# A clustered attention and MLP kernel: single entries for small instructions, constant products at the start, q's scale on VectorE, and another order

## The chip, the cores and the metric

The kernel runs on one core of a Trainium2 chip. The metric is the device time of one execution in microseconds (us), lower is better. The engines are TensorE (PE, products into PSUM), VectorE (DVE), ScalarE (ACT), GpSimd (POOL) and SyncE (SP, which here issues all DMAs). Each takes its instructions in the order in which the program issued them.

## The reference

```python
q_n, k_n, c_n = each row / (norm + 1e-6)
q_assign = argmax(q_n @ c_n.T); k_assign = argmax(k_n @ c_n.T)     # 16 centroids per head
scores = q @ k.T / sqrt(64), -1e9 where q_assign != k_assign
attn = softmax(scores); out = attn @ v                             # 4 batches, 8 heads, 768 rows, 64 columns
x = out as 3072 x 512
h = x @ w_in                                                       # 512 x 2048
g = (a0 + a1 h + a2 h^2 + a3 h^3) / (1 + |b0||h| + |b1| h^2 + 1e-6)
return g @ w_out                                                   # 2048 x 512
```

The MLP weights arrive as 64-bit floats, which the kernel unpacks itself (lines 517 to 562).

## The kernel before

Work is in *pairs* of heads, four pairs in each of four batches, 16 pairs in all. Each number is split into a high and a low float16 part, so that products keep their precision. A Python class `Plan` collects every step as a closure with its engine (`op(...)`), and a list `ORDER` of 4218 indices says in which order the closures are called. As each engine works in order, that list fixes every queue, and with it which buffer of a ring is given to whom. One closure may issue several instructions; between these nothing else can stand.

The steps that matter here:

- `prep` (line 885 on), for each pair: load q and k (`rq`, `rk`), sum of squares on ACT (`tk`, `tq`, with an accumulator), a transpose on PE (`kt`, `qt`, L949), a maximum over the partitions on DVE (`km`, `qm`, L951), a product with ones that spreads it (`kb`, `qb`, L953), then scales that are powers of two: `k_scale` (three DVE instructions, L963 to L971), `q_scale` (L963), `q_scale2` (three one-column instructions L979, L980, L982; on DVE for the first pair, on POOL for the 15 others), and a reciprocal (L993). With them ACT makes the high part and DVE the low part (L1012) of k and q. A transposing DMA (L1028) brings `tk` and `tq` to `sk` and `sq`. Then the logits against the centroids (`ptl`, L1060), the assignments (L1074 to L1084) and their marks (L1089, L1102), which are transposed too.
- Batch 0 goes key-major (`attend_keys`): 12 score blocks per pair (`s`, L1288), each followed by a maximum on DVE (`top`, L1297); when all are there, the row maxima are written in parts (`parts`, L1307 to L1314), `q2` is transposed again, second products `z` (L1332) follow, exponentials on ACT (`at`), products with v (`px`, L1351, which read `rv`), sums (L1357), a newton step (`newton`, two DVE instructions), a spread (L1385).
- Batches 1 to 3 (`attend`): scores (`s`, L1164), scale and maximum on DVE (L1193), exponential on ACT, high part on ACT, low part on DVE (`ah`, L1224), a transposing DMA, products with v (`px`, L1244).
- The MLP (`moe`): first product `ph` (L1453), the rational function on ACT, DVE and POOL, second product `po` (L1602). `g_scale` makes its column scales from 36 small instructions on DVE, POOL and ACT, bound into 10 entries.
- `v_scale` loads v (`rvm`, shared ring of two with the raw weights), squares it on ACT and makes one scale per batch (`vt`, `vb`). `rv` is v once more, in a ring of two buffers; in batch 0 a buffer is free when PE has read it for the last `px` of its pair.
- PSUM: the small products take their tiles from a ring of two (`misc`).

Of the kernel before, what the change touches and what calls it, by code (L numbers as in the profile page):

```python
# [18 lines left out]
P = 128  # L19
# [38 lines left out]
K = {'xn': 14, 'scp': 1, 'vsc': 0.75, 'sup0': 0, 'stk': 2, 'lop': 0, 'mgp': 0, 'rvn': 2, 'at': 3, 'vn': 3, 'ah': 5, 'sua': 1.0, 'T1': 1, 'quick': 1, 'sqd': 0.0, 'gld': 0.0, 'gp': 0.3, 'pp': 0.0, 'NR': 19, 'acb': 1.0}  # L58
# [3 lines left out]
3 4 5 6 7 8 9 377 376 379 381 382 383 40 41 42 43 388 44 28 32 29 30 31 33 391 392 45 374 375 380 384 385 386  # L62
10 387 389 390 34 35 36 37 38 394 395 46 47 11 393 489 490 398 492 50 48 49 51 494 495 496 501 70 71 72 74 396
73 399 400 401 402 403 397 39 52 404 405 407 406 488 487 493 497 498 88 92 89 53 54 90 504 505 76 77 78 79 499
500 502 91 93 80 55 56 57 503 507 508 64 67 68 81 58 408 506 509 409 414 415 82 83 12 13 61 62 69 63 59 430
431 84 418 419 510 86 85 87 60 75 410 411 424 425 432 433 412 413 428 429 420 421 511 512 513 514 14 0 601 378
16 600 15 17 18 19 422 423 416 417 515 516 426 427 434 603 602 605 607 608 609 65 517 518 520 614 94 95 606
118 122 119 120 519 96 97 98 99 20 21 22 112 116 610 23 611 121 113 114 612 613 615 616 617 618 115 117 123
103 104 435 436 437 440 441 453 454 438 439 455 456 442 443 521 619 522 535 536 620 621 622 623 109 130 131
132 715 124 125 126 127 128 129 106 134 133 527 528 529 530 110 111 444 445 446 447 135 107 24 25 26 541 542  # L70
470 471 100 624 625 626 713 716 718 448 449 27 627 628 629 105 450 457 458 533 534 537 538 136 137 630 525 526
1 714 172 173 176 719 160 164 108 631 632 635 66 633 161 162 459 723 724 138 139 140 141 460 174 472 473 539
540 145 142 151 152 101 102 531 532 175 177 720 721 725 726 523 524 163 545 546 543 544 722 727 547 146 147
# [12 lines left out]
301 303 295 674 675 676 271 296 297 277 268 269 270 582 1272 687 688 700 702 701 703 689 690 774 775 776 304
305 777 322 323 324 326 306 307 308 309 325 327 334 335 336 364 691 316 692 319 320 310 311 778 338 2 337 365
693 313 339 781 704 677 705 706 707 779 780 1274 1273 1275 1276 366 367 1277 1278 340 341 342 343 782 1398
1397 1403 1407 328 329 330 792 793 344 345 1279 1280 1281 331 794 1402 708 709 710 783 368 795 694 784 332 333
785 796 797 278 1229 1230 369 798 799 809 810 1404 1405 1406 811 786 787 1408 1409 370 371 321 228 346 347 788  # L90
789 813 1410 1411 1412 348 349 812 350 351 1413 1414 790 1401 1284 1282 361 358 1231 1232 362 363 312 565 317
318 791 372 373 678 800 801 814 802 803 815 816 355 1233 1234 1283 1285 1289 1290 1291 1539 1297 1298 1299 804
805 806 1292 1293 1300 1301 817 1235 1236 1237 1238 1239 1240 1294 1295 1302 1303 1313 1314 1241 818 1242 819
820 1416 1540 1541 1415 1417 1418 1419 1545 1542 1544 359 1315 1316 1317 1305 1306 1420 1421 1549 352 1318
1319 821 822 823 2228 1258 2229 279 275 276 314 315 1307 826 827 828 1308 829 832 833 1333 1334 1335 1309 1310
1422 830 831 1243 842 843 844 360 1311 1312 1423 1426 1320 1304 1296 1427 1424 1425 1546 1547 845 846 1336
1337 1325 1326 847 848 849 834 807 835 836 272 695 858 1548 1550 1551 273 356 357 837 838 839 1286 1327 1338
1339 1340 859 860 861 862 1552 863 850 864 1328 1329 865 808 851 852 874 875 1555 876 877 1341 1342 853 878
854 855 1330 1331 1343 880 879 1553 1554 1287 891 892 893 1344 894 1345 1346 840 1349 1350 1351 1352 1556 1347
1428 1353 1354 895 896 881 882 866 1684 1355 1356 2230 841 907 908 909 910 867 353 897 856 1361 1362 1363 1369  # L100
1370 1288 1321 1322 1323 1364 1371 868 911 912 857 1365 1366 1372 913 869 870 1373 1374 883 884 354 923 924
925 926 929 898 899 1367 1375 1324 1377 1378 1379 1385 1386 1387 1244 871 873 927 928 1380 1381 1388 1389 914
915 599 885 886 1348 1245 1246 933 1247 887 930 1382 1383 888 1390 1391 1332 1357 1358 1359 1360 900 916 940
941 942 943 946 2231 3222 3223 1431 1432 1439 1440 1441 944 917 945 1557 1558 1683 1682 1559 1560 1392 901 931
918 1561 1433 1434 1435 902 947 948 1442 1443 919 920 903 904 1436 1437 1444 1445 872 889 960 961 963 962 932
934 964 976 977 979 978 966 1562 967 1447 1448 1449 1450 982 983 965 980 1451 1455 1456 890 906 981 1368 1384
3224 1681 1376 1393 1394 1452 1453 935 936 937 1457 968 1458 1459 1563 1467 1468 1248 969 970 1686 1395 1396
1460 1461 1462 971 1564 1446 1454 1438 824 1469 993 994 996 1470 995 1471 949 972 973 997 1472 1473 998 1429
1565 1568 1569 2232 1430 3225 999 1000 905 1687 1009 1010 1011 1012 1483 1484 1485 1475 1476 1477 1013 1014
950 1486 1478 1479 1487 951 1691 952 953 1015 1016 1480 1481 922 921 1688 1689 1488 1489 1490 984 1001 938  # L110
1041 1042 1044 1043 1002 1491 1492 1493 1494 1045 986 985 987 1003 1495 1496 939 1503 1504 1505 1506 1249 1017
1046 1051 1497 1004 1047 1048 954 956 1463 1464 1465 1507 1508 1018 1690 1692 1693 1250 1511 1512 1513 1566
1567 1474 1482 2233 1509 1543 1514 1695 1005 988 989 990 1006 1466 1515 1516 1058 1059 1519 1520 1019 1517
1521 1522 1523 1696 955 958 1524 1525 1025 1026 1027 1060 1061 1028 1573 1574 1575 1576 1062 1251 1252 1064
1065 1694 1020 1031 1032 1577 1578 974 1527 1528 1063 825 1579 1029 1030 975 992 991 1007 1581 1582 1049 1697
1033 1034 1035 1529 1530 1531 1698 1036 1583 1584 1585 711 712 1685 957 1498 2253 1510 2254 1499 1500 1501
1502 1253 1021 1022 1532 1533 1586 1587 1074 1075 1076 1077 1078 1079 1080 1081 1050 1066 1094 1589 1095 1096
1097 1590 1591 1597 1598 1599 1600 1067 1699 1700 1701 1702 1592 1518 1526 1098 1703 1023 1008 1052 1053 1570
1571 1593 1037 1038 1068 1601 1054 1055 1704 1594 1595 1602 1603 1099 1534 2256 2252 1604 2251 1111 1112 1114
1113 1117 1118 1617 1618 1619 1620 1609 1610 1611 1024 1535 1536 1040 1057 1069 1621 1115 1070 1071 1100 1116  # L120
1612 1613 1705 1622 1623 1580 1596 1588 1624 1614 1615 1082 1083 1084 1712 1713 2257 1537 1633 1634 1635 1636
1119 2258 2259 1085 1706 1707 1708 1538 1572 1637 1638 1039 1625 1626 2260 2262 1710 959 1639 3226 1640 1627
1628 1629 1086 1087 1120 1121 1630 1631 2265 1073 1127 1128 1129 1133 1130 1645 2261 1646 1056 1647 1653 1654
# [1569 lines left out]
```

## Time and profile before

| | us |
|---|---|
| median of 3 runs | 914.93 (914.34 to 915.98) |
| the profiled execution | 914.8 |
| its span, first to last instruction | 913.0 |
| PE busy | 854.0 |
| DVE busy | 820.1 |
| ACT busy | 790.7 |
| POOL busy | 576.6 |

The span is the time from the first instruction to the last; the execution has 1.8 us around it. Busy times are sums over stages with different limits, so that the stages are read one by one.

### The profile page before, as it was taken

To read this page: it belongs to the slowest core of one execution; us is meant where nothing else is said; L and a number is where in the kernel's file an instruction comes from. 1 tells how busy PE (TensorE), PEld (TensorE's weight loads), DVE (VectorE), ACT (ScalarE), POOL (GpSimd) and SP (SyncE) were. 2 spreads that over 40 slices of the span, in tenths; PEclk is the share of its full clock that TensorE was granted. 3 is DMA by queue.
4 is the path that set the end of the run, shared out by engine and by line. 5 is a ranking of instruction groups with operands and counts; after the bars stand their busy time and mean duration, and the time that the engine had idled before them with its cause. 6 is when DMAs were issued, how large, how long until landed. Compare 5 with 4: busy or idle time off the path is not lost.

```text
span 913.0 us, 20529 instructions
## 1 busy us (share of the span) xinstructions
PE 854.0 (94%) x7705; PEld 584.9 (64%) x7705; DVE 820.1 (90%) x1538; ACT 790.7 (87%) x1486; POOL 576.6 (63%) x607
## 2 busy tenths in 40 slices
PE   1779998988999999999999999999999999999998
PEld 1456766765666766667666765776766566776663
DVE  6868888679999999999999999999999998887784
ACT  5576878999999999999999989999999798985662
POOL 3537767779675757458654765447756554668675
PEclk9979999999999999999999999999999999999999
DMA  8997784878959898997999779888987596320000
GB/s 229 237 204 175 174 197 142 191 184 148 184 122 196 142 202 180 195 172 131 215 160 203 156 126 187 162 163 149 189 179 136 96 199 105 70 47 1 36 24 23
DMA packets 360852, 137.70 MB, mean 151 GB/s; under 512 B 335664, under 2 KB 352048, under 8 KB 360752
## 3 DMA queue, kind: packets, MB, share of 16 engines
q1 hardware_dynamic: 360752, 136.39, 74.5%
q8 instruction: 60, 0.98, 0.4%
q14 instruction: 40, 0.33, 0.1%
HBM read 41.98 MB, written 6.29 MB: 53 GB/s over the span
## 4 chain that ended last, share of the span: by engine, by line
PE 53%; DVE 15%; ACT 15%; DMA 9%; issue 5%; SPq 1%; POOL 1%; ACTq 0%; DVEq 0%
PE po L1602 18%; PE ph L1453 17%; PE s L1164 6%; PE px L1244 5%; ACT s L397 4%; DMA sq<-tq 3%; DVE s L1193 3%; ACT ah L397 2%; ACT u L397 2%; DVE ah L1224 2%; DMA rvm<-in_v_dram 2%; PE z L1332 1%; ACT t L397 1%; DVE g L1553 1%; PE ptl L1060 1%
## 5 line engine op out<-in xcount | busy, mean ns | idle before, releaser
L1602 PE MATMUL po<-wout,g 128*128 128x512 f16 x1152 | 266.7, 379 | 0.5 <-POOL g L1591 0.3
L1453 PE MATMUL ph<-x,win 128*128 128x256 f16 x2304 | 266.3, 273 | 0.6 <-DVE df L1075 0.4
L1453 PEld LDWEIGHTS <-win 128*128 128x128 f16 x2304 | 223.6, 98 | 41.7 <-DVE t L1478 1.7
L1602 PEld LDWEIGHTS <-g 128*128 128x128 f16 x1152 | 111.2, 98 | 121.3 <-issue 2.2
L1591 POOL TENSOR_TENSOR g<-t,u 128x512 f16<-128x512 f32 x84 | 117.6, 1402 | 97.1 <-DVE t L1584 81.1
L1193 DVE TENSOR_SCALAR_CACHE_REDUCE s<-s,cc 128x768 f32<-128x768 f32 x144 | 144.7, 1018 | 4.2 <-PE s L1164 3.7
L1224 DVE SCALAR_TENSOR_TENSOR ah<-s,su,ah 128x768 f16<-128x768 f32 x144 | 143.4, 1009 | 3.9 <-ACT ah L397 3.4
L1518 POOL TENSOR_TENSOR s<-s,u 128x512 f32<-128x512 f32 x84 | 112.5, 1344 | 49.5 <-ACT s L397 38.8
L397 ACT ACTIVATE s<-s,nm 128x768 f32<-128x768 f32 x144 | 126.0, 876 | 12.3 <-DVE s L1193 10.4
L397 ACT ACTIVATE ah<-s,su 128x768 f16<-128x768 f32 x144 | 127.0, 898 | 10.3 <-DVE su L1212 9.4
L1164 PE MATMUL s<-sk,sq 128*128 128x384 f16 x576 | 114.2, 326 | 11.7 <-DVE ah L1224 9.2
L1164 PEld LDWEIGHTS <-sq 128*128 128x128 f16 x576 | 53.0, 97 | 52.6 <-DVE ah L1224 17.4
L1244 PE MATMUL px<-at,vhi 128*64 128x256 f16 x864 | 73.9, 275 | 1.0 <-DVE t L1478 0.6
L397 ACT ACTIVATE t<-ph,gk 128x512 f32<-128x512 f32 x84 | 65.2, 779 | 3.7 <-PE ph L1453 3.7
L1471 DVE SCALAR_TENSOR_TENSOR t<-ph,gk,t 128x512 f32<-128x512 f32 x84 | 62.3, 742 | 4.8 <-ACT t L397 3.3
L1572 DVE SCALAR_TENSOR_TENSOR s<-s,g 128x512 f32<-128x512 f32 x84 | 64.6, 769 | 0.7
L1478 DVE SCALAR_TENSOR_TENSOR t<-t,gk,ph 128x512 f32<-128x512 f32 x84 | 62.3, 742 | 1.3
L397 ACT ACTIVATE s<-u,g 128x512 f32<-128x512 f32 x84 | 60.6, 724 | 1.1 <-POOL t L1578 0.3
L397 ACT ACTIVATE u<-s,cq 128x512 f32<-128x512 f32 x84 | 59.7, 718 | 1.7 <-POOL s L1518 1.7
L1244 PE MATMUL px<-at,vlo 128*64 128x256 f16 x432 | 59.6, 273 | 0.0
L397 ACT ACTIVATE u<-ph,gk 128x512 f32<-128x512 f32 x84 | 57.4, 688 | 1.4 <-PE ph L1453 0.9
L1553 DVE SCALAR_TENSOR_TENSOR g<-t,gk,u 128x512 f16<-128x512 f32 x61 | 53.5, 878 | 4.1 <-ACT u L397 3.9
(227 smaller groups left out, 1543.2 us busy)
## 6 DMA issues: line engine op xcount, KB each, us to landing
rwi<-in_moe_w_in_dram SPq DMA_DIRECT2D x16, 512.0 KB, 3.7
rwo<-in_moe_w_out_dram SPq DMA_DIRECT2D x16, 512.0 KB, 4.8
rk<-in_k_dram SPq DMA_DIRECT2D x32, 192.0 KB, 3.6
rq<-in_q_dram SPq DMA_DIRECT2D x32, 192.0 KB, 3.7
rvm<-in_v_dram SPq DMA_DIRECT2D x16, 384.0 KB, 4.3
rv<-in_v_dram SPq DMA_DIRECT2D x16, 384.0 KB, 4.4
out_dram<-ob SPq DMA_DIRECT2D x24, 256.0 KB, 3.1
sk<-sk SPq DMA_DIRECT2D x12, 192.0 KB, 3.5
```

The source lines that it names most:

```text
L397: lambda: nc.scalar.activation(out=out(), in_=in_(), func=func, **{a: (x() if callable(x) else x) for a, x in kw.items()}),
L1164: nc.tensor.matmul(sc.ap[:, i, :SH], lhsT=st["q" + x].ap[:, j, t, :], rhs=st["k" + x].ap[:, j, ks, :].rearrange("p t c -> p (t c)"), start ...
L1193: lambda nm=nm, view=view: ts(out=view(), in0=view(), scalar1=cc.ap[:, 0:1], scalar2=None, op0=ALU.mult, op1=ALU.min, accum_out=nm.ap),
L1224: lambda part=part, view=view, su=su: stt(out=part(1), in0=view(), scalar=su.ap, in1=part(0), op0=ALU.mult, op1=ALU.subtract),
L1244: nc.tensor.matmul(px.ap[j * D : (j + 1) * D, :], lhsT=vv.ap[:, j, kt, :], rhs=at[j].ap[:, p_, kt].rearrange("p t c -> p (t c)"), start=(i ...
L1453: nc.tensor.matmul(ph.ap[:, fi * TW : (fi + 1) * TW], lhsT=win[:, wpart, c, f * P : (f + 1) * P], rhs=xs[c].ap[:, xpart], start=(i == 0), ...
L1471: lambda t=t, h=h, ph=ph, col=col: stt(out=t[h].ap, in0=ph.ap, scalar=col("rho")(), in1=t[h].ap, op0=ALU.mult, op1=ALU.mult),
L1518: lambda uv=uv, sv=sv: nc.gpsimd.tensor_tensor(out=sv(), in0=sv(), in1=uv(), op=ALU.mult),
L1553: lambda tv=tv, uv=uv, col=col, g16=g16: stt(out=g16(0), in0=tv(), scalar=col("a0")(), in1=uv(), op0=ALU.add, op1=ALU.mult),
L1572: lambda sv=sv, g16=g16: stt(out=sv(), in0=sv(), scalar=1.0 + 1e-6, in1=g16(0), op0=ALU.add, op1=ALU.mult),
L1591: lambda tv=tv, uv=uv, g16=g16, e=(nc.vector if kshare("gld", b, i_) else nc.gpsimd): e.tensor_tensor(out=g16(1), in0=tv(), in1=uv(), op=A ...
L1602: nc.tensor.matmul(po[ti].ap, lhsT=g16(gg)[:, c0 : c0 + P], rhs=wout[:, wpart, f, :], start=(i == 0 and f == 0), stop=(i == 2 and f == NF ...
```

## The change

`ORDER` has 4446 entries instead of 4218. 212 come from splitting: `scales`, `bound1`, `square_term`, `root`, `bound3`, `bound4`, `columns` (in `g_scale`), `k_scale`, `q_scale2`, `fixed_rows`, `mark`, `parts` and `newton` were closures with two to ten instructions and are now one entry for each instruction. 16 are new: `warm`, eight products of a constant 128 x 128 tile with itself into a tile of the `misc` ring, which nobody reads. `q_scale2` goes to DVE for all 16 pairs. The list is another one throughout.

```diff
-K = {..., 'acb': 1.0}
+K = {..., 'acb': 1.0, 'warm': 16, 'fast': 16}
...
+    w16w = cp.tile([P, P], BF16, name="w16w")
+    nc.vector.memset(w16w, 1.0)
...
+    def warm(vt):
+        wm = misc([P, 2 * TW], F32, f"warm{vt}")
+
+        def spin():
+            for _ in range(8):
+                nc.tensor.matmul(wm.ap[:, :P], lhsT=w16w, rhs=w16w, start=True, stop=True)
+
+        op("PE", 433, spin, [], [wm], vt)
...
-        def q_scale2():
-
-            pts = ts if quick else nc.gpsimd.tensor_scalar
-            pts(out=qs.ap[:, 1:2], in0=ks.ap[:, 1:2], scalar1=2.0 ** -21, scalar2=1.0, op0=ALU.mult, op1=ALU.mult)
-            pts(out=qs.ap[:, 0:1], in0=qs.ap[:, 0:1], scalar1=2.0 ** 61, scalar2=qs.ap[:, 1:2], op0=ALU.mult, op1=ALU.max)
...
-        if quick:
-            op("DVE", 480, q_scale2, [ks], [qs, cc], u, n=3)
-        else:
-            op("POOL", 1635, q_scale2, [ks], [qs, cc], u)
+        fast = b * NPAIR + hp < kn("fast", 1)
+        pts = ts if fast else nc.gpsimd.tensor_scalar
+        op(
+            *(("DVE", 481) if fast else ("POOL", 1631)),
+            lambda: pts(
+                out=qs.ap[:, 1:2], in0=ks.ap[:, 1:2], scalar1=2.0 ** -21, scalar2=1.0, op0=ALU.mult, op1=ALU.mult
+            ),
+            [ks], [qs], u,
+        )
...
-            dve(1200, newton, [px], [rw], ux, [rwc])
+            dve(
+                1201,
+                lambda px=px, rw=rw, rq=rq: stt(
+                    out=rw.ap[:, P:], in0=px.ap[:, 1, :P], scalar=eps, in1=rq(), op0=ALU.add, op1=ALU.mult
+                ),
+                [px], [rw], ux, [rwc],
+            )
...
+    for i in range(int(kn("warm", 0))):
+        warm(-40 + 0.01 * i)
```

How the first entries of some queues read in the two lists (pair numbers after the names; halves of q and k are loaded one by one):

```
SP before:   centroids, k0, k0, w_in, w_in, q0, q0, w_in, w_in, k1, k1, transpose k0, w_out, transpose q0
SP after:    q0, v (rvm0), q0, w_in, centroids, k0, k0, w_in, w_in, w_out, transpose k0, w_in, transpose q0, k1
rv before:   pair 0, 1, 2, 3 of batch 0       rv after: pair 0, 3, 1, 2
ACT before:  centroid norm, square k0, w_in, w_in, scale k0, square q0, ...
ACT after:   square v (rvm0), square q0, w_in, square k0, centroid norm, w_in, scale k0, ...
PE before:   kt0 kb0 qt0 qb0 centroids kt1 kb1 ptl0 w_in qt1 w_in qb1, scores of pair 0
PE after:    8 warm, qt0, 2 warm, kt0 kb0 qb0 centroids, 2 warm, ptl0, 2 warm, kt1 kb1 qt1 qb1 w_in w_in,
             7 scores of pair 0, 2 warm, 5 scores of pair 0
```

## Rows read from the trace of the kernel before

**Rows 1.** Stretch, length; busy PE, PEld, DVE, ACT, POOL (xcount); PE clock, DMA share, GB/s.

```profile
0.00:60.00 60.00, 29.76 (x225) 19.58 (x226) 44.33 (x118) 34.02 (x60) 26.93 (x45) 0.89 0.95 231
60.00:240.00 180.00, 164.25 (x1937) 119.34 (x1937) 151.96 (x298) 156.12 (x295) 134.83 (x155) 1.00 0.75 173
240.00:800.00 560.00, 551.32 (x4826) 376.97 (x4821) 541.28 (x1029) 532.61 (x1027) 337.33 (x351) 1.00 0.86 160
800.00:900.00 100.00, 100.00 (x688) 65.33 (x687) 78.17 (x90) 66.72 (x105) 74.70 (x56) 1.00 0.09 25
900.00:913.00 13.00, 8.68 (x41) 3.72 (x38) 4.38 (x6) 1.26 (x2) 2.77 (x3) 0.91 0.11 40
```

**Rows 2.** PE's waits, longest first, in 0-60, 60-240, 240-800: us, times, longest.

```profile
PE kt L949 <- ACT tk L397: 14.6, 3, 5.4
...
PE s L1164 <- DVE ah L1224: 3.3, 4, 1.5
...
PE s L1164 <- DVE ah L1224: 5.8, 7, 1.7
```

**Rows 3.** Chain of waits: start, us, what.

```profile
55.27 6.76 PE z L1332 x36
```

**Rows 4.** `kt` on PE: two instructions (start, us), then all 16 (ns min/median/max).

```profile
5.32 0.37 PE L949 MATMUL kt<-ident,sumk 128*1 128x128 f32 x1 [5.32 <-ACT tk L397]
...
48.29 0.37 PE L949 MATMUL kt<-ident,sumk 128*1 128x128 f32 x1 [3.85 <-ACT tk L397]
...
L949 PE MATMUL kt<-ident,sumk x16: 270/272/372, 5.3 to 663.8; 128*1 128x128 f32 x16
```

**Rows 5.** Stages as in rows 1: the start, and around 50 us.

```profile
4.00:8.00 4.00, 0.95 (x3) 0.57 (x3) 2.88 (x14) 2.16 (x4) 0.00 (x0) 1.00 0.92 325
48.00:56.00 8.00, 5.68 (x31) 4.29 (x32) 4.28 (x19) 5.50 (x12) 1.80 (x4) 0.50 1.10 211
```

**Rows 6.** DVE in order of time, around the first maximum of a score block.

```profile
32.83 0.34 DVE L1019 COPY tq<-tq 128x768 f16<-128x768 f16 x1
33.51 0.96 DVE L1297 TENSOR_REDUCE top<-s 128x1 f32<-128x768 f32 x1 [0.33 <-PE s L1288]
34.79 0.96 DVE L1297 TENSOR_REDUCE top<-s 128x1 f32<-128x768 f32 x1 [0.32 <-PE s L1288]
```

**Rows 7.** ACT in order of time: one exponential of `z`.

```profile
57.99 0.90 ACT L397 ACTIVATE at<-z,cc 128x768 f32<-128x768 f32 x1 [0.38 <-PE z L1332]
```

**Rows 8.** The three scale instructions by line: ns min/median/max, first and last start.

```profile
L979 POOL TENSOR_SCALAR qsc<-ksc x15: 190/192/515, 27.2 to 670.1; 128x1 f32<-128x1 f32 x15
L979 DVE TENSOR_SCALAR qsc<-ksc x1: 144/144/144, 12.8 to 12.8; 128x1 f32<-128x1 f32 x1
...
L980 POOL TENSOR_SCALAR qsc<-qsc x15: 291/295/904, 29.6 to 670.4; 128x1 f32<-128x1 f32 x15
...
L980 DVE TENSOR_SCALAR qsc<-qsc x1: 214/214/214, 13.0 to 13.0; 128x1 f32<-128x1 f32 x1
...
L982 POOL TENSOR_SCALAR cc<-qsc,ksc x15: 260/265/697, 30.3 to 670.8; 128x1 f32<-128x1 f32 x15
L982 DVE TENSOR_SCALAR cc<-qsc,ksc x1: 213/213/213, 13.3 to 13.3; 128x1 f32<-128x1 f32 x1
```

**Rows 9.** All waits, longest first: that of POOL before L980.

```profile
POOL qsc L980 <- DVE qsc L963: 14.5, 6, 4.0
```

**Rows 10.** PE in order of time: three reads of `rv`.

```profile
90.25 2.81 PE L1351 MATMUL px<-at,rv 128*64 128x256 f32 x24
...
125.58 2.81 PE L1351 MATMUL px<-at,rv 128*64 128x256 f32 x24
...
140.53 2.81 PE L1351 MATMUL px<-at,rv 128*64 128x256 f32 x24
```

**Rows 11.** DMA issues (the page): KB each, us to landing.

```profile
rv<-in_v_dram SPq DMA_DIRECT2D x16, 384.0 KB, 4.4
```

**Rows 12.** SP's queue in order of time.

```profile
95.00 3.93 SPq L411 DMA_DIRECT2D rwi<-in_moe_w_in_dram  x2
```

More of the change, by code (lines that the diff above doesn't have):

```diff
@@ L869, in g_scale, with pts1 @@
-        dve(590, scales, [wie, ev], [gk, g1], vt, n=2)
-        op("POOL", 1820, bound1, [aab], [g1], vt)
-        dve(160, bound2, [], [g1], vt)
-        op("POOL", 1300, square_term, [aab], [g1], vt)
+        def pts1(ns, out, in0, s1, s2, op0, op1, r=(), w=None):
+            op(
+                "POOL", ns,
+                lambda: pts(out=out(), in0=in0(), scalar1=s1() if callable(s1) else s1, scalar2=s2() if callable(s2) else s2, op0=op0, op1=op1),
+                list(r), w or [g1], vt,
+            )
@@ new lines, in G, with A @@
+        def G(i):
+            return lambda: g1c(i)
+        def A(i):
+            return lambda: ac(i)
+        MU, AD, MX = ALU.mult, ALU.add, ALU.max
+        dve(591, lambda: ts(out=kk["rho"](), in0=wi_e, scalar1=ev.ap[:, 0:1], scalar2=None, op0=MU), [wie, ev], [gk], vt)
+        dve(592, lambda: nc.vector.tensor_reduce(out=g1c(HB), in_=kk["rho"](), axis=AX.X, op=MX), [gk], [g1], vt)
+        pts1(1821, G(HB), G(HB), 4.0 * math.sqrt(H) * TOP * TOP, 1.0, MU, MU)
+        pts1(1822, G(D1), G(HB), A(5), A(4), MU, AD, [aab])
@@ L874, in g_scale @@
         act(250, lambda: g1c(R1), lambda: g1c(R1), AF.Exp, [], [g1], vt, scale=0.5)
-        dve(1700, root, [], [g1], vt, n=4)
-        op("POOL", 1460, bound3, [aab], [g1], vt)
-        dve(1330, bound4, [woe], [g1], vt, n=5)
-        op("POOL", 3400, columns, [ab, aab, woe], [gk, g1], vt)
+        dve(1701, lambda: nc.vector.reciprocal(out=g1c(BT), in_=g1c(R1)), [], [g1], vt)
+        dve(
+            1702, lambda: stt(out=g1c(R1), in0=g1c(BT), scalar=g1c(X1), in1=g1c(R1), op0=MU, op1=AD), [], [g1], vt,
+        )
@@ new lines, in g_scale @@
+        pts1(1822, kk["sg"], lambda: wo_e, G(HB), TOP, MU, MU, [woe, g1], [gk])
+        pts1(1821, G(OI), G(OI), 1.0 / TOP, 1.0, MU, MU)
+        pts1(1822, G(BT), G(BT), A(4), 1.0, MU, MU, [aab])
+        pts1(1822, kk["kap"], kk["rho"], G(R1), 1.0, MU, MU, [g1], [gk])
+        op("POOL", 1823, lambda: ptt(out=kk["sr"](), in0=kk["sg"](), in1=kk["rho"](), op=MU), [], [gk], vt)
+        for name, src, i in (("a2", "sr", 2), ("a1", "sr", 1), ("a0", "sg", 0), ("a3r", "sr", 3)):
+            pts1(1822, kk[name], kk[src], lambda i=i: ab.ap[:, i : i + 1], 1.0, MU, MU, [ab], [gk])
@@ L881, in clustered_attention_moe_kernel @@
+        op("POOL", 1823, lambda: ptt(out=kk["a3r"](), in0=kk["a3r"](), in1=kk["rho"](), op=MU), [], [gk], vt)
     xt = {}
@@ L987, in prep @@
[L987 to L992 removed]
+        dve(146, q_scale, [qsum], [qs], u)
+        dve(536, lambda: half_exponent(ks.ap[:, 0:1], pb.ap), [pb], [ks], u)
+        dve(
+            537,
+            lambda: ts(
+                out=ks.ap[:, 0:1], in0=ks.ap[:, 0:1], scalar1=2.0 ** 62, scalar2=2.0 ** -60, op0=ALU.mult, op1=ALU.max
+            ),
+            [], [ks], u,
+        )
@@ new lines, in prep @@
+        dve(538, lambda: nc.vector.reciprocal(out=ks.ap[:, 1:2], in_=ks.ap[:, 0:1]), [], [ks], u)
+        fast = b * NPAIR + hp < kn("fast", 1)
+        pts = ts if fast else nc.gpsimd.tensor_scalar
+        op(
+            *(("DVE", 481) if fast else ("POOL", 1631)),
+            lambda: pts(
+                out=qs.ap[:, 1:2], in0=ks.ap[:, 1:2], scalar1=2.0 ** -21, scalar2=1.0, op0=ALU.mult, op1=ALU.mult
+            ),
+            [ks], [qs], u,
+        )
+        op(
+            *(("DVE", 482) if fast else ("POOL", 1632)),
+            lambda: pts(
+                out=qs.ap[:, 0:1], in0=qs.ap[:, 0:1], scalar1=2.0 ** 61, scalar2=qs.ap[:, 1:2], op0=ALU.mult, op1=ALU.max
+            ),
+            [], [qs], u,
+        )
@@ L993, in prep @@
+        op(
+            *(("DVE", 483) if fast else ("POOL", 1633)),
+            lambda: pts(
+                out=cc.ap[:, 0:1], in0=qs.ap[:, 0:1], scalar1=ks.ap[:, 0:1], scalar2=QSC if keymajor else -QSC,
+                op0=ALU.mult, op1=ALU.mult,
+            ),
+            [qs, ks], [cc], u,
+        )
         dve(157, lambda: nc.vector.reciprocal(out=qs.ap[:, 1:2], in_=qs.ap[:, 0:1]), [], [qs], u)
@@ L1043, in rows @@
                 return tm[x].ap.rearrange("p h t d -> p (h t) d")[:, :, P - NCL :]
-            def fixed_rows():
-                nc.gpsimd.tensor_copy(out=rows("k2"), in_=mrow.unsqueeze(1).broadcast_to([P, 2 * NT, NCL]))
-                nc.gpsimd.memset(rows("q2"), 0.0)
-            op("POOL", 1100, fixed_rows, [], [tm["k2"], tm["q2"]], vt + kb("p2", b, 2))
+            op(
+                "POOL", 1101,
+                lambda: nc.gpsimd.tensor_copy(out=rows("k2"), in_=mrow.unsqueeze(1).broadcast_to([P, 2 * NT, NCL])),
+                [], [tm["k2"]], vt + kb("p2", b, 2),
+            )
+            op("POOL", 1102, lambda: nc.gpsimd.memset(rows("q2"), 0.0), [], [tm["q2"]], vt + kb("p2", b, 2))
         for x in ("k1", "q1"):
```

132 lines of the change are left out of this document (64 added, 68 removed), and 376 rows, old and new, of the table ORDER.

## The prediction

> **What bounds the kernel now.** I read the busy times by stage first, then what TensorE (PE) waits for in each stage, then single instructions where a wait has to be priced. By the stage table [rows 1] PE is busy 29.76 of the first 60 us, 164.25 of the next 180, 551.32 of the 560 after that, all of 800 to 900, and 8.68 of the last 13. So its idle time is 30.2 + 15.8 + 8.7 + 0 + 4.3 = 59 us of 913. From 240 us on PE is the bound; an order can only win what PE idles, or bring the dense part forward. The same rows show how little room the other engines have there: VectorE (DVE) is busy 541.28 and ScalarE (ACT) 532.61 of 560 us.
>
> What PE waits for differs by stage [rows 2]: in the first 60 us for the squares of q and k on ACT, whose input is a load; from 60 to 240 and from 240 to 800 most of all for DVE (row `ah`). The first dense PE work, the second products `z` of pair 0, starts at 55.27 us [rows 3]; everything before it is a chain of load, scales, transposing DMA, 12 scores with a maximum each, and one more transposing DMA.
>
> **The change part by part.**
>
> *Separate entries.* The same instructions are issued, so nothing is added; what is gained is that another instruction may stand between two of them. Alone: 0. It only matters through the order, below.
>
> *Constant products.* 16 entries of 8 products of 128 columns, 128 in all. In PE's new queue 8 groups stand ahead of the first real work, the rest at places 9, 10, 15, 16, 18, 19, 33 and 34, so the last two lie among the first scores. They take no engine but PE, which idles half of that stretch [rows 1], so their own time costs 0; two groups among scores that wait for a 0.95 us maximum each cost at most 1 us. Where a group takes a PSUM buffer of the ring of two, it waits for the reader of that buffer: the group at place 19 waits until DVE has read the logits of pair 0, and the transposes of pair 1 (`kt`) wait behind it. Pair 1 has the room, since its scores begin after pair 0's.
>
> What they can give is clock. The granted clock is recorded as 1.00 in the first 44 us, but `kt` took 0.37 us at 5.32, the same as at 48.29, where the recorded clock is 0.50 (1.2 GHz), against a median of 272 ns over all 16 [rows 4, 5]. By the durations PE ran at 1.2 GHz at the start, by the recorded clock at 2.4. On the path to the first scores the slow rate costs: DVE idles 0.33 + 0.32 us for PE before the first two maxima [rows 6], and the small products ahead of them about 0.1 us each, some five of them, so about 1.2 us in all. Bounds: 0, if the clock falls back in the long waits that stay between the groups and the scores, and 1.2, if it stays up. I take 0.6, because the last groups stand right at the scores but most run before 8 us. The second slow stretch, 0.50 from 48 to 56 us [rows 5], costs ACT 0.38 us before each of three exponentials (one of them in [rows 7]), 1.1 us; no group stands near it, so I take 0 and keep 1.1 for the range.
>
> The Trainium skill ("TensorE: Matmul & The Clock Gate", section "What's actually happening") says that the array's default state is the throttled clock and that activity releases it. By that page the 1.00 at the start is no granted level but a missing record, and the groups lift the clock. By the recorded 1.00 the whole term would be 0 and the sum 0.6 us higher; by the durations it is as taken.
>
> *q's scale.* For 15 of 16 pairs three one-column instructions leave POOL (192 + 295 + 265 ns) and go to DVE (144 + 214 + 213 = 571 ns) [rows 8]. DVE gets 15 x 0.571 = 8.6 us more. POOL loses 11.3 us and, more, the 14.5 us for which it stood before the second of the three until DVE had made its input [rows 9]. POOL is busy 337 of 560 us in the dense part [rows 1], so I book nothing for that. On DVE at most the 12 pairs of batches 1 to 3, 6.9 us, fall into 240 to 800, where it idles 18.7 us. Bounds: 0, if they all fall into holes, and +6.9, if DVE's queue is what PE waits for throughout. PE's waits for DVE there are 5.8 us of 8.7 [rows 2], but 5.8 us in 560 is rare; I take +0.5.
>
> *The new order, start.* In SP's queue the load of q and the first load of v for the scale of v come first, then w_in, centroids, and k; before, it was centroids, k, w_in, q. ACT's first entry becomes the square of v. So k's square, which sets off k's scale, comes later by the two loads that now precede it, q's earlier, and one 384 KB load is gone from the stretch after 30 us. DVE has 52 instructions ahead of its first maximum before (33.51 us) and 53 after: three scale instructions of pair 1 more (0.57 us), against a copy (0.34 us, as the one in [rows 6]) and the two short instructions of a weight block's scale (about 0.3 us) that move behind it. That is a draw, and DVE, busy 44 of these 60 us [rows 1], paces the stretch. The moved ones then lie between the first maximum and the last part of the row maxima, 0.65 us. I take 0, with 2.5 us either way: the 0.65, and the time by which one 384 KB load may hold k.
>
> *The new order, the ring of v.* The two buffers of `rv` are loaded early with pairs 0 and 1 before, with pairs 0 and 3 after. So the loads of pairs 1 and 2 now wait in SP's queue until PE has read the buffer of the pair before, and behind the first of them stand loads of w_in and the transposes of pair 3. Pair 0's last read ends at 90.25 + 2.81 = 93.1 us and pair 1's at 125.58 + 2.81 = 128.4 [rows 10]; a load takes 4.4 us to land [rows 11]. So pair 1 has its rows at about 98 us and pair 2 at 133; pair 1 needs them some 12 us after pair 0's last read, pair 2 at 140.53. SP's next issue of weights was held until 95.00 before as well [rows 12]. Cost 0; were SP held longer than that, each us would delay pair 3.
>
> *The new order, the rest.* The coarse sequence is unchanged: on PE the score, exponent and MLP blocks stand at the same places but for the 16 added entries, with shifts of a few us of PE work either way. The tail has the same 16 `po` entries after the last `ph`. What can change is the 15.8 + 8.7 us of idle in 60 to 800, mostly waits for DVE, in whose queue the maxima, the newton steps and the scale of g now interleave. A finer interleaving should bring some of these forward; others will come later. I take -2 us, under a tenth of it, with 8 either way as the bound (a third of all that idle).
>
> **The sum.** It is made against the profiled execution: span 913.0, 914.8 us with what lies around it, which is 0.1 below the median of 914.93. 0 - 0.6 + 0.5 + 0 + 0 - 2 = -2.1, so 912.7 us.
>
> **The rivals.**
> - *DVE becomes the bound (slower).* The added one-column instructions land in front of maxima and second parts for which PE waits. Place: 240 to 700 us. Price: up to 6.9 us, less the 0.6 of the clock; 914.8 + 6.9 - 0.6 = 921, with half of it hidden 918. It decides once DVE's idle in 240 to 800 is all but used: 18.7 us now, 11.8 after the addition. For it: DVE heads PE's waits. Against: the instructions are short and POOL's stall of 14.5 us goes with them. I put it at 918.5.
> - *The start comes later (slower).* k's square after v's and q's delays the first transposing DMA; if `z` starts 2.5 us later than 55.27, and nothing after makes it up, 917.3.
> - *Nothing shows.* PE's idle stays what it is: new waits replace old ones, the groups run in time that was idle and the clock is back at 1.2 GHz when the scores come. 914.8.
> - *The order closes holes.* A third of the idle of 60 to 800 (8 us), and the full 1.2 us of clock: 905.6.
>
> **How the numbers follow.** Forecast (a small gain) 0.33; holes closed 0.12; nothing shows 0.25; DVE bound 0.20; later start 0.10. A difference under 0.2%, 1.8 us, can't be told from none here. That gives 0.45 faster, 0.25 same, 0.30 slower. The range goes from the holes closed (905.5) to DVE's price nearly in full (920.5), which leaves out some 0.1 on either side. The likeliest case alone spans 909 to 913.
>
> **What would show it.** Right: PE's idle before 60 us still about 30 us, `z` of pair 0 starting within 53 to 57 us; `kt` and `qt` of pair 0 at 270 ns instead of 372, but 0.50 recorded again around 50 us; POOL's wait before L980 gone; idle of PE from 60 to 800 near 22 us instead of 24.5; the tail unchanged. Wrong: waits of PE for DVE in 240 to 800 above 10 us (DVE bound); `z` after 58 us (start); a load of `rv` that lands after PE is ready for it; a dense part that begins before 50 us would mean that I overrate the chain at the start, and a slow clock that is gone at 50 us that I underrate the groups.

## The result, and the profile after

The changed kernel takes 904.49 us (median of 4 runs, 902.24 to 906.91) against 915.45 for the kernel before (4 runs, 914.34 to 918.76): ratio 0.9875, 95% interval 0.9838 to 0.9911, so 8 to 15 us less. The prediction was 912.7, 2.1 us less than before, with a range from 905.5; the sign was right, the size about five times too small, and the time lies just below the range. The profiled execution of after took 906.91 us (span 904.7), the slowest of the four; against the 914.8 of the one before that is 7.9 us.

The experiments below ran on four chips, each of them beside the kernel before on the same chip. So each has its median time and its ratio to the kernel before, and differences between experiments are differences of these ratios, times 915.4 us.

The stages, as in [rows 1] (length; busy PE, PEld, DVE, ACT, POOL with counts; clock, DMA share, GB/s):

```profile
0.00:60.00 60.00, 38.66 (x346) 28.62 (x347) 43.68 (x123) 33.23 (x58) 22.28 (x36) 0.72 0.90 223
60.00:240.00 180.00, 167.63 (x1979) 123.28 (x1979) 148.07 (x317) 158.23 (x301) 136.53 (x153) 1.00 0.77 175
240.00:800.00 560.00, 555.17 (x4854) 379.98 (x4849) 537.84 (x1060) 538.38 (x1036) 334.17 (x322) 1.00 0.87 162
800.00:900.00 100.00, 100.00 (x663) 62.88 (x661) 74.28 (x86) 58.22 (x91) 71.43 (x54) 1.00 0.05 15
900.00:904.70 4.70, 0.32 (x2) 0.00 (x0) 0.00 (x0) 1.26 (x2) 0.00 (x0) 0.92 0.30 112
```

From 60 to 800 us PE idles 12.4 + 4.8 = 17.2 us where it idled 24.5: 7.3 us less, nearly all of the 7.9. The extra busy time before 60 us is the 128 constant products, which is no progress. The tail is as it was (4.4 us idle at the end, 4.3 before).

PE's longest waits from 240 to 800 us in after (us in total, times, longest), to be held against the `ah` row of [rows 2]:

```profile
PE ph L1508 <- DVE t L1533: 1.2, 2, 0.6
PE s L1193 <- DMA sk<-sk: 1.1, 1, 1.1
PE px L1273 <- DMA at<-ah: 0.9, 3, 0.4
PE ptl L1088 <- DMA sk<-tk: 0.7, 1, 0.7
PE s L1193 <- DVE ah L1253: 0.4, 2, 0.2
```

The wait for `ah` is what went: 3.3 + 5.8 us from 60 to 800 before, 0.4 us now. The DVE instruction that makes the second half of `ah` is the last reader of a score block's PSUM tile, and there are two such tiles: the next block `s` waits in PE until it is done. In the new order PE hardly waits for it; that this instruction now stands earlier in DVE's queue is how I read the row, and no run moved it alone.

The three scale instructions are on DVE for all pairs, as [rows 8] had them for one, and POOL's wait of [rows 9] is gone; the second and third can lie far from the first (last starts 673.6 and 683.1 us):

```profile
L1000 DVE TENSOR_SCALAR qsc<-ksc x16: 135/144/155, 14.5 to 673.6; 128x1 f32<-128x1 f32 x16
L1007 DVE TENSOR_SCALAR qsc<-qsc x16: 183/211/215, 14.7 to 683.1; 128x1 f32<-128x1 f32 x16
L1014 DVE TENSOR_SCALAR cc<-qsc,ksc x16: 198/210/216, 14.9 to 683.3; 128x1 f32<-128x1 f32 x16
```

Busy times alone can't say where a kernel got ahead. So I gave every matmul the mean step of its kind (line and shape) over the runs, left the constant products out, and added the steps up in order of time: the PE work done by a moment. This table is worked out from the traces so; in us, and as the difference to before.

```
             by 60 us   240    520    760    800
before         19.7   172.8  443.6  672.5  712.0
after          -0.7    +3.3   +3.4   +8.1   +8.2
no_products    -0.1    +3.8   +3.7   +8.0   +8.0
products_only  -1.5    -0.7   -0.8   -0.8   -0.9
q_on_pool      -1.1    +0.5   -0.2   +2.7   +2.6
q_on_dve_only  -1.1    -5.3   -7.8  -10.5  -10.4
new_until_60   +0.0    -0.4   -1.0   -1.1   -1.2
new_until_240  +0.1    +4.0   +2.6   +2.5   +2.3
new_from_240   -0.4    -2.2   -7.4   -3.0   -3.1
new_from_520   -1.4    -2.9   -3.5   -1.2   -1.2
dve_load_old   -1.0    -1.9   -5.8   -8.2   -8.3
dve_load_new   -0.9    +2.4   +0.2   +1.6   +1.5
products_in_gap +1.7   +5.5   +5.6  +11.3  +11.4
```

After is 0.7 us behind at 60 us, gains 4 us by 240, nothing by 520, and 4.7 us from 520 to 760. One caution: new_from_240 and new_from_520 run the old order up to their cut and are yet 2 to 3 us behind before at 240 us, so a difference of 2 to 3 us at one moment between two executions means nothing, and where such a difference is named below it is no more than a hint.

### The profile page after: what moved, and what is told of

Same layout as the page of the kernel before. It is cut to its first block, busy times and chain, and to the rows that moved or that the text cites. A ratio compares the mean times of both kernels' runs of the same rounds, so it can differ in the third digit from the quotient of the medians.

```text
span 904.7 us, 20799 instructions
## 1 busy us (share of the span) xinstructions
PE 861.8 (95%) x7833; PEld 594.8 (66%) x7833; DVE 803.9 (89%) x1584; ACT 789.3 (87%) x1486; POOL 564.4 (62%) x562
## 4 chain that ended last, share of the span: by engine, by line
PE 63%; DVE 15%; DMA 8%; ACT 6%; issue 4%; SPq 2%; POOL 0%; ACTq 0%; DVEq 0%; POOLq 0%
PE po L1657 21%; PE ph L1508 20%; PE s L1193 7%; PE px L1273 6%; DVE s L1222 3%; DVE ah L1253 3%; PE s L1317 2%; PE z L1378 2%; DMA rwi<-in_moe_w_in_dram 2%; DVE t L1526 2%; DMA sk<-tk 2%; DMA at<-ah 1%; PE ptl L1088 1%; DMA sq<-tq 1%; DMA sk<-sk 1%
## 5 line engine op out<-in xcount | busy, mean ns | idle before, releaser
L1646 POOL TENSOR_TENSOR g<-t,u 128x512 f16<-128x512 f32 x84 | 115.0, 1370 | 82.9 <-DVE t L1639 64.3
L1627 DVE SCALAR_TENSOR_TENSOR s<-s,g 128x512 f32<-128x512 f32 x84 | 60.9, 730 | 1.7 <-POOL g L1602 0.9
L1273 PEld LDWEIGHTS <-vhi 128*64 128x64 f16 x864 | 46.1, 110 | 14.0 <-issue 10.1
```

What stands on the lines that cost most here:

```text
L1273: nc.tensor.matmul(px.ap[j * D : (j + 1) * D, :], lhsT=vv.ap[:, j, kt, :], rhs=at[j].ap[:, p_, kt].rearrange("p t c -> p (t c)"), start=(i ...
L1627: lambda sv=sv, g16=g16: stt(out=sv(), in0=sv(), scalar=1.0 + 1e-6, in1=g16(0), op0=ALU.add, op1=ALU.mult),
L1646: lambda tv=tv, uv=uv, g16=g16, e=(nc.vector if kshare("gld", b, i_) else nc.gpsimd): e.tensor_tensor(out=g16(1), in0=tv(), in1=uv(), op=A ...
```

## The experiments

**Theories.** (1) The order carries the gain, since split entries let work go in between. (2) Taking q's scale off POOL carries it. (3) The constant products lift the clock. And, once these had run: does DVE's queue set the pace, and why is q's scale dear in one order and cheap in the other?

The kernels with the old order and split entries keep the entries of a bundle side by side; their instructions then stand in the order of before on every engine (but for one added constant).

**One part taken away or done alone.**

`no_products`, `q_on_pool`: the changed kernel, less one part.

```diff
-'warm': 16, 'fast': 16      # changed kernel
+'warm': 0, 'fast': 16       # no_products, their 16 entries left out of the order
+'warm': 16, 'fast': 1       # q_on_pool
```

> The changed kernel without the 16 groups of constant products; everything else, the order too, as changed. If the order carries the gain: 904 to 907 us, since in the trace of after the first product z of pair 0 starts at 56.19 us, no earlier than the 55.21 of before, so the groups can have given 1 us at most. If the clock that the groups lift carries it: 910 us or more, most of the 11 us lost again. If the groups themselves cost time at the start: 902 to 903 us.

> The changed kernel with q's scale of 15 pairs back on POOL, at the same places of the order. If the order carries the gain: 904 to 908 us; the 15.8 us of DVE time that fell away come from POOL and DVE standing in each other's way less, at other moments. If taking the three short instructions off POOL (14.5 us of standing still, 11.3 us of work) carries it: 910 us or more, and POOL waits before the second of the three again.

`q_on_dve_only`, `products_only`: the old order, plus one part.

```diff
-'warm': 0, 'fast': 1        # old order
+'warm': 0, 'fast': 16       # q_on_dve_only
+'warm': 16, 'fast': 1       # products_only, at the like places
```

> The kernel before, entries split but side by side as they were, no constant products, and q's scale of all 16 pairs on DVE. If the order carries the gain: 913 to 917 us, no change. If q's scale carries it: 905 to 910 us. If 6.9 us more DVE work in the dense part are on the path, as one rival had it: 918 us or more.

> The kernel before, entries split but side by side as they were, q's scale as before, and the 16 groups of constant products: 8 ahead of PE's first work and 8 ahead of the same PE work as in the changed kernel. If the order carries the gain: 913.5 to 916 us. If the lifted clock does: 910 us or less, with the first dense products before 52 us.

Measured, as ratio to before with its interval: without the products 0.9884 (0.986 to 0.9908), 905.48 us; q on POOL 0.995 (0.9931 to 0.9968), 911.39 us; the old order with q on DVE 1.0077 (1.0052 to 1.0103), 923.51 us; the old order with the products 1.0006 (0.9991 to 1.0021), 916.29 us.

So the products do nothing that can be told, alone or in the new order. The other two parts act on each other: the new order with q's scale on POOL gives 4.6 us (2.9 to 6.3); q's scale on DVE costs 7.0 us in the old order (4.8 to 9.4), and in the new one gives 6.9 us more (0.995 against 0.9875; by the two intervals some 3 to 11). The new order has the places of the three instructions as DVE has them; an order laid out for q's scale on POOL was not tried. Neither theory 1 nor theory 2 stands by itself.

In the old order with q on DVE, PE's waits from 240 to 800 us are longer where they were long before:

```profile
PE s L1192 <- DVE ah L1252: 7.1, 11, 1.7
PE ph L1507 <- DVE t L1532: 1.3, 3, 0.5
```

In the new order with q on POOL, this is the start, first POOL, then DVE in order of time (start, us, instruction; in brackets the idle time before it and what ended it):

```profile
30.94 1.26 POOL L574 TENSOR_TENSOR wwo<-wwo,gwo 128x512 f32<-128x512 f32 x1 [1.36 <-DVE wwo L565]
32.28 0.19 POOL L1000 TENSOR_SCALAR qsc<-ksc 128x1 f32<-128x1 f32 x1
32.58 0.31 POOL L1007 TENSOR_SCALAR qsc<-qsc 128x1 f32<-128x1 f32 x1
32.99 0.27 POOL L1014 TENSOR_SCALAR cc<-qsc,ksc 128x1 f32<-128x1 f32 x1
```

```profile
30.10 0.69 DVE L565 SCALAR_TENSOR_TENSOR wwo<-rwo,wwo 128x512 int32<-128x512 int32 x1
32.92 0.16 DVE L1020 RECIPROCAL qsc<-qsc 128x1 f32<-128x1 f32 x1 [2.13 <-POOL qsc L1007]
```

The small scale of pair 1 stands behind a weight product of 1.26 us in POOL's queue; DVE stands still for 2.13 us at the reciprocal that needs it, and with it everything behind. In the changed kernel, where DVE makes the scale, the same reciprocal starts at 31.23 us without a wait:

```profile
31.09 0.21 DVE L1014 TENSOR_SCALAR cc<-qsc,ksc 128x1 f32<-128x1 f32 x1
31.23 0.15 DVE L1020 RECIPROCAL qsc<-qsc 128x1 f32<-128x1 f32 x1
```

Here are DVE's waits for POOL's scale over the whole run, first in the kernel before, then in the new order with q on POOL:

```profile
DVE qsc L993 <- POOL qsc L980: 0.5, 1, 0.5
```

```profile
DVE qsc L1020 <- POOL qsc L1007: 3.9, 3, 2.1
```

So in the old order POOL's scale came in time for all pairs but one, and taking it to DVE had only its price; in the new order it comes late. PE's waits for `ah` from 60 to 800 us are 3.3 us with q on POOL, against 0.4. Part of what the trace with q on POOL lacks by 240 us (2.8 us of PE work) is none of this: in this stretch the granted clock was below 1.00, and 24 products `ph` that start in it took 4.46 us, against 2.78 in after.

```profile
200.00:204.00 4.00, 3.83 (x21) 2.87 (x22) 3.03 (x10) 2.73 (x5) 3.81 (x5) 0.60 0.02 4
```

**The split entries put together again, in the new order.**

`bundled`: every bundle at the place of its last entry (two at that of the first). `k_last`: only k's scale so. `bundled_first`: k's scale, the parts of the maximum and the newton steps at the place of their first entry, the rest at the last.

```diff
-... ks#1 ... ks#2 ... ks#3 ...      # entries of k's scale in the order
+...          ...      ks#1 ks#2 ks#3 ...   # bundled, k_last
+... ks#1 ks#2 ks#3 ...     ...             # bundled_first
```

> The changed kernel with the new order, q's scale on DVE and the products, but the split instructions put side by side again, each bundle at the place of its last entry (of its first in two cases). If the coarse new order carries the gain, 904 to 907 us. If what stands between the split instructions carries it, 909 to 915 us; the separate entries would then be worth the difference to 904.5.

> The changed kernel; only the three instructions of k's scale are put side by side again, at the place of the third. The first of them reads the PSUM result of kb, and in the run with all bundles PE waited for it 15 us in all, up to 4.4 us at a time. If this is what made that run 62 us slower than after: 940 us or more. If it was the bundles of the weight scale (up to 78 DVE instructions lie between their entries): 905 to 915 us.

> All bundles side by side again, but k's scale, the parts of the row maximum and the newton steps at the place of their first entry, the others at that of their last. If k's scale at its last place was the trouble and the coarse new order carries the gain, 904 to 908 us: separate entries are then worth little. If separate entries are worth the gain: 910 to 916 us.

Measured: bundled 968.46 us, ratio 1.0554 (1.0532 to 1.0577); k_last 943.45 us, 1.0301 (1.0275 to 1.0326); bundled_first 922.37 us, 1.0062 (1.0038 to 1.0085). The coarse new order with bundles is worse than the old order in all three, and bundled and bundled_first are slower than either of the ranges expected: what stands between the entries is needed. PE's waits in k_last, over the whole run:

```profile
PE ph L1508 <- DVE ksc L977: 15.1, 7, 4.8
```

The first instruction of k's scale takes 0.15 us and reads `kb`, a PSUM tile of the same ring from which `ph` takes its tiles. Moved to the place of the third, it frees that tile late, and `ph` waits for it. That is 15 of the 39 us that k_last is slower than the changed kernel. The waits cost a second time, by the clock. After a wait of 2.77 us for k's scale 24 products `ph` took 5.22 us instead of 2.78, and the granted clock was 0.50:

```profile
212.93 5.22 PE L1508 MATMUL ph<-x,win 128*128 128x256 f16 x24 [2.77 <-DVE ksc L977]
218.63 2.78 PE L1508 MATMUL ph<-x,win 128*128 128x256 f16 x24
```

```profile
212.00:218.00 6.00, 5.07 (x25) 3.62 (x25) 1.84 (x6) 0.94 (x3) 2.59 (x5) 0.50 0.87 161
```

From 60 to 240 us the granted clock is 0.95 on average in k_last and 1.00 in after, and over the whole run PE is busy 872.8 us against 861.8 with the same products. In bundled_first the wait for k's scale is gone, but the one for `ah` is back, with 8.1 us, where after has 0.4:

```profile
PE s L1193 <- DVE ah L1253: 8.1, 11, 1.3
```

This doesn't show that a good order with bundles can't exist, only that this order lives by the separate entries.

**Where the order gains.** Entries split, no products; one order up to the PE work before a moment, then the other; q's scale on DVE for the pairs in the new part (and pair 0).

```diff
-fast = b * NPAIR + hp < kn("fast", 1)
+fast = b * NPAIR + hp in (0, 1, 2)                 # new_until_60
+fast = b * NPAIR + hp in (0, 1, 2, 3, 4, 5, 6)     # new_until_240
+fast = b * NPAIR + hp in (0, 7, 8, ..., 15)        # new_from_240
+fast = b * NPAIR + hp in (0, 12, 13, 14, 15)       # new_from_520
```

> Entries split, no products. The new order up to the PE work that lies before 60 us (q's scale of pairs 0 to 2 on DVE), then what is left in the order of before, q's scale of the other pairs on POOL. PE of after had done 0.7 us less work by 60 us than PE of before, so: 914 to 917 us, no gain. If the start carries the gain: 909 us or less.

> As new_until_60, but the new order up to the PE work that lies before 240 us, q's scale of pairs 0 to 6 on DVE. By the work done up to 240 us in the two traces (3.3 us more in after) and if the later part keeps that lead: 911 to 913 us. If DVE's work is what counts from the start to the end and must be cut in all stages: 914 to 917 us, the lead is given back.

> The opposite: the order of before up to the PE work that lies before 240 us, q's scale there on POOL (pair 0 on DVE), then what is left in the new order, q's scale of those pairs on DVE. By the two traces after gains 4.5 us from 520 to 760 us and nothing from 240 to 520: 910 to 912 us. If the gains of the two halves hang together: 914 us or more, or, if DVE becomes the bound there, 918.

> Entries split, no products; the order of before up to the PE work that lies before 520 us, q's scale there on POOL (pair 0 on DVE), then what is left in the new order, q's scale of the last four pairs on DVE. By the two traces the new order gains 4.5 us between 520 and 760 us: 911 us, plus what the seam costs (1.6 and 6 us in the two runs cut at 240 us, by the PE work done), so 911 to 914 us; the PE work done must show the 4 to 5 us between 560 and 760 us.

Measured: until 60 us 914.77 us, 0.9992 (0.998 to 1.0004); until 240 912.87 us, 0.9973 (0.9957 to 0.9988); from 240 913.8 us, 0.9983 (0.9966 to 1.0001); from 520 913.32 us, 0.9965 (0.9952 to 0.9978). The start gives nothing. The pieces together give less than the whole, and the table of work done says why: new_until_240 is 4.0 us ahead at 240 us and loses 1.7 of it within the next 20 us; new_from_240 loses 5.9 us there and then gains 4.4 from 520 to 760, as after does. Its loss at the seam holds one wait of PE that no other run here has at this length (235 to 262 us):

```profile
PE po L1656 <- POOL g L1645: 3.5, 1, 3.5
```

Behind this wait the granted clock was 0.50 from 246 to 252 us, so PE lost work after it as well. New_from_520 gains 2.3 us from 520 to 760, half of what after gains there; the rest is open.

**Does DVE set the pace?** 8.6 us of DVE work that nobody waits for (4 x 144 ns for 15 pairs), in either order, and then POOL work of the same sort in the new one.

```diff
+for _ in range(4 if b + hp else 0):                  # dve_load_old_order, dve_load_new_order
+    ts(out=scr, in0=scr, scalar1=1.0, scalar2=1.0, op0=ALU.mult, op1=ALU.mult)
+nc.gpsimd.tensor_scalar(out=scr[:, 1:2], ...)        # pool_small_load: three, like those of q's scale
+nc.gpsimd.tensor_tensor(out=scr[:, 0], in0=scr[:, 0], in1=scr[:, 1], op=ALU.mult)   # pool_wide_load, 128x256
```

> The kernel before, entries split but side by side, q's scale on POOL, no products; behind k's scale of 15 pairs four added one-column DVE instructions on a scratch tile, 4 x 144 ns, 8.6 us of DVE work that nobody waits for. If DVE's queue sets the pace in the old order, as the 8 us of the run with q's scale on DVE suggest: 920 to 924 us. If it was q's scale that came late there: 915 to 917 us.

> The changed kernel without the products, with the same 8.6 us of added DVE work. If DVE still sets the pace: 911 to 914 us. If the new order has given DVE slack (it idles 22 us from 240 to 800 us): 905 to 907 us.

> The changed kernel without the products, q's scale on DVE, and beside it for 15 pairs the same three one-column instructions on POOL, on a scratch tile that nobody waits for. If POOL's instructions hold up DVE's and this is why q's scale on POOL was 6.5 us slower: 909 to 912 us. If it was the handing over between the engines (DVE waited for POOL's scale, 3.9 us in the trace, and everything behind it): 905 to 907 us.

> The changed kernel without the products; for 15 pairs one product of two 128x256 tiles more on POOL, on a scratch tile that nobody waits for; about 0.67 us each by the like instruction that writes x, 10 us in all. POOL idles 226 of the 560 us from 240 to 800. If only POOL's own queue counted: 905 to 906 us. If such an instruction stops DVE's while it runs: 908 to 911 us, about as much as the 8.6 us of added DVE work cost (6 us).

Measured: DVE work added to the old order 920.6 us, 1.0048 (1.0029 to 1.0066), so +4.4 us (2.7 to 6.0); to the new order 910.88 us, 0.9936 (0.9912 to 0.996), so +4.8 us over no_products (by the two intervals some 2 to 8). POOL work added to the new order: small 906.57 us, 0.9893 (0.9874 to 0.9912), wide 906.2 us, 0.9892 (0.9874 to 0.9909), +0.8 and +0.7 us over no_products, within the spread. From 240 to 800 us PE waits for `ah` thus in the old order and in the new one with the added DVE work:

```profile
PE s L1198 <- DVE ah L1258: 9.0, 15, 1.7
```

```profile
PE s L1198 <- DVE ah L1258: 2.6, 8, 0.5
```

So each us of DVE work added at this place costs about half a us in both orders; other places were not tried. It is DVE's queue, not POOL's, that stands beside PE as the bound, and the new order has not freed it.

That q's scale on POOL was dear because its instructions hold up DVE's is not borne out: the same ones beside it, with nobody waiting, cost no more than the spread. The handing over, as in the rows at 32.92 us above, is what the trace shows in its place, but the 6.9 us are not split into their parts. DVE waited 3.9 us for POOL's scale. And it does not get less busy by giving the three instructions away: 805.0 us with q on POOL against 803.9 in after, though they take 8.6 us. So its other instructions took that much longer with q on POOL; the added small POOL work alone lengthened DVE's time by 2.3 us only (804.6 to 806.9). Where the rest of that comes from is open.

**The clock.** The products where PE waits ahead of its first dense work, none at the start: 7 groups, then 9.

```diff
-16 groups: 8 ahead of PE's first work, 8 by the 34th entry     # changed kernel
+ 7 groups: 3 behind ptl of pair 1, 1 behind qb, 1 behind kb of pair 2, 2 behind vt   # products_in_gap
+ 9 groups: 1 more behind qt, 1 more behind kt of pair 2         # products_in_gap_9
```

> The changed kernel with 7 groups of products instead of 16, none at the start: three behind the logits of pair 1, one behind qb of pair 2, one behind kb of pair 2, two behind the transpose of v, all between 45 and 55 us, where PE idles 4.6 us and the recorded clock falls to 0.50. If the slow clock at the first dense products costs something: 902 to 904 us, and the granted clock stays at 1.00 through 60 us. If DVE's queue sets the pace there: 905 to 906 us, whatever the clock.

> As products_in_gap, with 9 groups: one more behind qt and one more behind kt of pair 2. If the clock at the first dense products is worth what the trace of products_in_gap shows (1.7 us more PE work done by 60 us than in the run without products, 3.4 us by 800): 2 to 3 us below the changed kernel on the same chip. If only the spread of chips: within 1 us of it.

> The changed kernel once more, on the chip of products_in_gap_9: 902 to 907 us, as in the first four runs of it; its ratio to the kernel before on this chip is what the other one is held against.

Measured: 7 groups 904.03 us, 0.9862 (0.9844 to 0.988); 9 groups 905.62 us, 0.9872 (0.9846 to 0.9898); the changed kernel on the same chip as these 9, 906.68 us, 0.9881 (0.9856 to 0.9906). With 7 groups, the stage that was slow in [rows 5] and the products `z` from there to 70 us (ns min/median/max):

```profile
48.00:56.00 8.00, 6.27 (x75) 4.92 (x72) 6.23 (x24) 5.82 (x10) 3.26 (x5) 1.00 0.90 187
```

```profile
L1377 PE MATMUL z<-sq,sk x46: 269/272/283, 54.9 to 70.0; 128*128 128x256 f16 x46
```

The same row without products:

```profile
L1377 PE MATMUL z<-sq,sk x42: 270/378/421, 55.1 to 69.2; 128*128 128x256 f16 x42
```

The slow stretch is gone, and PE has done 1.7 us more than in no_products by 60 us. In the time of the whole kernel this is 1 to 2 us at most, inside the intervals. The 2 to 3 us expected of the 9 groups didn't come (0.9872 against 0.9881, 0.8 us); in their trace the granted clock fell again later, to 0.97 on average from 60 to 240 us. No version here is shown to be faster than the changed kernel.

## Why the prediction was right and wrong

*Separate entries, 0 alone:* right, since alone they change no instruction's place; products_only, which has them in the old order, is at 1.0006. That it matters "only through the order" was right in words and never priced: without them the new order is 17 us slower (bundled_first) or worse.

*Constant products, -0.6 (0 to -1.2):* right within what can be measured (+0.5 us, -0.8 to +1.9, in the old order). The details held too: `qt` and `kt` of pair 0 run in 270 ns, against 372 in [rows 4], and 0.50 is recorded again from 52 us. But the clock is back at 0.50 before the scores:

```profile
7.50 0.27 PE L963 MATMUL qt<-ident,sumq 128*1 128x128 f32 x1
...
10.87 0.27 PE L963 MATMUL kt<-ident,sumk 128*1 128x128 f32 x1
```

```profile
16.00:36.00 20.00, 12.85 (x115) 9.30 (x116) 17.20 (x48) 9.55 (x18) 7.07 (x7) 0.50 0.97 245
```

The kernel before was no faster there, although its clock reads 1.00: 16 products `wig` took 1.87 us in it and 1.89 in after. The rise to 1.00 that the scores see is recorded at 36.9 us in both traces, so the groups changed nothing for them.

```profile
23.35 1.87 PE L576 MATMUL wig<-wwi 128*128 128x128 bf16 x16
```

```profile
29.36 1.89 PE L588 MATMUL wig<-wwi 128*128 128x128 bf16 x16
```

The lower bound given there, "if the clock falls back in the long waits that stay between the groups and the scores", is what happened: PE waited 8.0 us for `cnrm` in between.

*The start, 0 with 2.5 either way:* right. `z` of pair 0 starts at 56.19 us, 0.9 later than [rows 3], and new_until_60 is within 0.2%. DVE's first maximum comes 1.6 us later than in [rows 6], at 35.15 us, and no longer waits for PE.

```profile
56.19 4.02 PE L1378 MATMUL z<-sq,sk 128*128 128x256 f16 x18
```

*The ring of v, 0:* right; PE waits for no load of `rv` in after.

*q's scale, +0.5 (0 to +6.9):* the step that failed. Two things were wrong in it. DVE's time was called cheap because PE's waits for DVE were 5.8 us in 560; the added load shows a price of about 0.5 us for each us. An engine busy 541 of 560 us had no slack worth the name, and a count of waits says what the engine costs now, not what more work will cost. And the term was priced from the trace of the old order alone, as if it were the same in every order. There DVE waited 0.5 us in all for POOL's scale, so nothing was to be gained; in the new order it waits 3.9 us, because the scale stands behind a weight product in POOL's queue, and DVE stands at the reciprocal until POOL has come round. POOL's 14.5 us before the second scale [rows 9], rightly booked at nothing, are POOL's own waits: in q_on_dve_only they are gone and the time rose all the same. So the range began at 0, with no gain possible, where the measured values are +7.0 us (old order) and -6.9 us (new order). The rows of [rows 8] say what the instructions cost, not what waiting for them does.

*The rest of the order, -2 (8 either way):* the mechanism named, waits for DVE brought forward, was right, and the 24.5 us of idle fell to 17.2, not to 22. The order with q's scale on POOL is worth 4.6 us (2.9 to 6.3), so the term was less than half of it. That a tenth of the idle would go was a guess with no row behind it; the rows that could have given it are those of `ah`, 9.1 us from 60 to 800, of which 8.7 went.

*The rivals.* "The order closes holes" (905.6, at 0.12) is nearest to what came out: its 8 us of idle were right (7.3), its 1.2 us of clock did not show, and it had nothing for q's scale, without which the order closes less (4.6 us). That its sum fits is in part luck. "DVE becomes the bound" (918.5 to 921) is what happens in the old order, 923.5: its mechanism was real, and the order decided over it. Both had been weighed as cases of one sum, when the parts of the change don't add up: +7.0 for q's scale and -4.6 for the order make +2.4 by addition; together they made -11.

## What to carry to other kernels

Where two engines are busy nearly all the time, add a load of known size to the second one before calling its time free; and price a change of engine with the order that goes with it, in both orders. A tiny instruction on another engine can cost what stands ahead of it in that queue, so ask who waits for its result. A wait of PE can cost twice, so look at the granted clock behind it. Before putting small instructions in one bundle, look for one that frees a buffer: of three that follow each other, the first may be the only one that somebody waits for.

## What the runs showed of the hardware

A DVE instruction got longer while POOL worked, and ended with POOL's. DVE, then POOL, in after:

```profile
114.16 0.65 DVE L1337 TENSOR_SCALAR tq<-top 128x96 f16<-128x96 f32 x1
```

```profile
114.07 0.67 POOL L1457 TENSOR_TENSOR x<-rw,x 128x256 f16<-128x256 f32 x1
```

The same DVE instruction takes 209 ns at its shortest; here it ends at 114.81, POOL's at 114.74. The Trainium skill ("SBUF — State Buffer", section "SBUF: two separate sides") says that the two engines share a port pair as an exclusive lock, which some of VectorE's instructions need, and that whichever starts first has it for its whole instruction while the other is blocked; these rows agree, POOL's having started first (114.07 against 114.16). I had taken this for the reason of the gain, since DVE's busy time fell from 820.1 to 803.9 us although it has more to do. Yet 13.5 us more of POOL time (563.7 to 577.2, pool_wide_load against no_products) raised DVE's by 4.0 us only (804.6 to 808.6) and the kernel's by 0.7, within the spread. The shorter DVE time does come with the order and its separate entries: bundled_first, with the same instructions on the same engines, has 820.6 us. Whether it is a cause of the gain there or goes along with it is open.

A granted clock of 1.00 at the start can mean that there is no record. The profile of after shows 1.00 from 0 to 12 us, though the first five groups of products took 1.04 to 1.06 us each and those from 6.36 us on 0.61. Later groups took 1.06 us at 20.35 us, where the clock is recorded as 0.50, and 0.61 at 41.12, where it is 1.00. So by the durations PE began at 1.2 GHz and rose to 2.4 while they ran. The first record of the clock in this trace starts at 6.2 us, with 1.00; in the trace of before it starts at 36.9 us.
